# Batch 0 of a linear attention is loaded and attended by halves of its heads

## The chip, the cores and the metric

The kernel runs on one core of a Trainium2 chip. The metric is the device time of one execution in microseconds (us). Three runs of the kernel before took 282.03, 282.73 and 283.08 us; the median is 282.73.

A core has five engines, each with its own queue of instructions: PE (TensorE: matmuls, and transposes as matmuls with an identity), DVE (VectorE), ACT (ScalarE), POOL (GpSimd) and SP (SyncE, here only an issuer of transfers). 16 DMA engines move data between the chip's memory and the on-chip memory. PE writes to eight banks of accumulators (PSUM), from which DVE and ACT read.

## The reference

A linear attention with cosine weights, followed by a two-layer network with the gate h·cos(h):

```python
batch, n_heads, seq, head_dim = (8, 8, 576, 64)
theta = np.pi / 2.0 * pos / S
def phi(x, c, s):
    r = np.maximum(x, 0.0)
    return np.concatenate([r * c, r * s], axis=-1)
q_p, k_p = phi(q, cos_w, sin_w), phi(k, cos_w, sin_w)
kv = np.einsum('bhsf,bhsd->bhfd', k_p, v)
z = np.sum(k_p, axis=2)
num = np.einsum('bhsf,bhfd->bhsd', q_p, kv)
den = np.einsum('bhsf,bhf->bhs', q_p, z)[..., None] + 1e-06
x = (num / den)          # transposed to (4608, 512)
h = x @ w_in             # 512 x 2048
return (h * np.cos(h)) @ w_out   # 2048 x 512
```

All inputs and the output are float32; the kernel computes in float16 with float32 sums.

## The kernel before

**Tiles.** A batch has 576 tokens: four tiles of 128 (t = 0 to 3) and a fifth of 64, which is computed together with the fifth tile of the neighbouring batch. Batches 0 and 1 are attended at the start; the others are attended while the network works on the batch before them.

**Attention of one batch**, as helper functions put it. `load` brings one of q, k, v by two transfers on SP's queue (lines 339 and 342), for a slice of heads. `prep` makes one feature (g = 0 cosine, g = 1 sine) of one token tile, on ACT (line 364) or DVE (line 365). `q_pe` transposes the q features of a tile, one transpose a head (line 420), and copies the bank to `qT`. `cast_v` casts v to float16 beside a column of ones (lines 378, 379). `kv` sums k features times v over the five tiles, four heads in each of two banks (line 391), and copies the sums to `kvz` (lines 404, 406). `num` multiplies `qT` with `kvz` (line 450), copies the denominators to `den` (468, 470), and its `norm` takes a reciprocal and multiplies (474, 476). `x_pe` transposes the result (line 496) into `xT`, the input of the network.

**The network of batches 0 and 1.** `layer1` makes 16 groups of eight matmuls (line 542). Each group needs two of the four token tiles of `xT` (hf = 0: tiles 0 and 1; hf = 1: tiles 2 and 3) and one of four quarters of w_in. A sine on ACT (line 514) and a product on DVE (line 519) follow each group. Three banks are used in turn. `layer2_plain` (line 784) then multiplies with w_out, first the lower half of the rows for all four tiles, then the upper half. Later batches use a scheme with fewer matmuls (lines 685 and 849) and sums on DVE.

**Order.** Each step is recorded with an engine and the keys that it reads and writes. The table `KEYS` gives each step a place; the steps are issued in the order of that table, so each engine's order is fixed. A step that may go to two engines has its choice in the last digit.

**The front.** `first_attention` clears the fifth tiles, runs 14 filler matmuls (`warm`, line 917) while the loads run, loads q and k whole and v by halves of the heads, and attends the batch with 16 more filler matmuls between the transposes of q and `kv`, and 4, 3, 2, 0 after the tiles' sums. `weights` (on POOL) waits for k (`hold`, line 922), then issues w_in's quarters 0, 2 and 1, waits for quarter 0 (`hold2`, line 932), and issues one of w_out's lower quarters, w_in's quarter 3 and the other one of w_out. Batch 1's loads wait on SP for small casts on POOL (`hold_raw`, line 947), which wait for w_in's quarter 0 and for whoever still reads batch 0's raw tile. The upper half of w_out waits for batch 1's q (`part_of_w_out`, line 954).

Of the kernel before, what the change touches and what calls it, by code (L numbers as in the profile page):

```python
# [10 lines left out]
AF = mybir.ActivationFunctionType  # L11
ALU = mybir.AluOpType
# [181 lines left out]
def kernel(  # L194
# [9 lines left out]
    nc = tc.nc  # L204
    B, H, S, D = q.shape
    Dm, Dff = moe_w_in.shape
    P = 128
# [886 lines left out]
```

## Time and profile before

| | us |
|---|---|
| median of three runs | 282.73 |
| the profiled execution | 281.65 |
| its span, first to last instruction | 279.2 |
| PE busy | 269.7 |
| DVE busy | 250.3 |
| ACT busy | 218.6 |
| first matmul of layer 1, batch 0 | 21.69 |
| first matmul with w_out | 37.77 |

The profile is of one execution, with times from the start of its span. The slices of the span show the busy share of each engine in tenths. A line of the chain of waits has a start, a length and an engine with a line of the kernel. A line of the timeline has a start, a length, engine, line, operation, output<-input and a count; behind it, in brackets, the idle time before it and what ended that. The granted clock is the share of its full clock that PE was given.

### The profile page before, as it was taken

The numbers are of one execution on the slowest core, as the hardware profiler recorded it, in microseconds if no ns is written. First come the engines' busy times: TensorE is split into PE (matmuls) and PEld (weight loads), VectorE is DVE, ScalarE is ACT, GpSimd is POOL, SyncE is SP. The second block draws the span as 40 slices with busy tenths as digits, with TensorE's granted clock in tenths as the row PEclk, the third lists the DMA queues.
The fourth block names the chain that finished last, engine by engine and source line by source line (L and its number), as shares of the span: only waits on it lengthen the run. The fifth ranks groups of instructions, "written<-read, shape, count | busy, mean of one in ns | idle before, by whom it ended". The sixth has DMA issues, their size and how long they took to land.

```text
span 279.2 us, 6855 instructions
## 1 busy us (share of the span) xinstructions
PE 269.7 (97%) x2715; PEld 218.8 (78%) x2715; DVE 250.3 (90%) x449; ACT 218.6 (78%) x401; POOL 8.4 (3%) x21
## 2 busy tenths in 40 slices
PE   7789999999999999999999999999999999999994
PEld 2558767769856778789879887998788888888883
DVE  2678699999999999999999999999999999998872
ACT  2756698799999999999999999984684686777210
POOL 1340020000000000000000000000000000000000
PEclk9799999999999999999999999999999999999999
DMA  6999999979999999999799999747210400200324
GB/s 199 316 196 252 250 319 268 338 201 171 332 300 245 241 251 273 308 218 260 233 283 233 285 252 243 155 78 206 40 39 4 188 2 0 77 0 2 150 79 150
DMA packets 77599, 53.30 MB, mean 191 GB/s; under 512 B 46080, under 2 KB 75264, under 8 KB 77568
## 3 DMA queue, kind: packets, MB, share of 16 engines
q1 hardware_dynamic: 72608, 48.12, 65.3%
q0 software_dynamic: 4224, 4.19, 9.1%
q10 hardware_dynamic: 736, 0.57, 0.6%
q8 instruction: 21, 0.34, 0.5%
q14 instruction: 10, 0.08, 0.1%
HBM read 36.74 MB, written 9.44 MB: 165 GB/s over the span
## 4 chain that ended last, share of the span: by engine, by line
PE 91%; DMA 3%; ACT 2%; DVE 2%; issue 0%; SPq 0%; ACTq 0%
PE M L849 34%; PE M L685 16%; PE M L542 10%; PE M L582 9%; PE TR L685 6%; PE M L784 5%; PE ATT L450 3%; PE ATT L391 3%; DMA km<-in_k_dram 3%; PE TR L582 1%; PE M L420 1%; ACT KQ L364 1%; PE M L917 1%; PE M L496 1%; ACT V L378 1%; DVE gT L519 1%
## 5 line engine op out<-in xcount | busy, mean ns | idle before, releaser
L514 ACT ACTIVATE ch<-M 128x512 f32<-128x512 f32 x90 | 54.0, 604 | 14.0 <-PE M L685 6.8
L849 PEld LDWEIGHTS <-gT 128*128 128x128 f16 x560 | 54.1, 98 | 8.2
L519 DVE TENSOR_TENSOR gT<-M,ch 128x512 f16<-128x512 f32 x84 | 55.8, 683 | 4.4 <-ACT ch L514 4.1
L849 PE MATMUL M<-w_out_sb,gT 128*128 128x256 f16 x448 | 56.4, 272 | 0.0
L364 ACT ACTIVATE KQ<-km,CS 128x512 f16<-128x512 f32 x56 | 39.0, 734 | 0.5 <-DMA km<-in_k_dram 0.5
L364 ACT ACTIVATE KQ<-qm,CS 128x512 f16<-128x512 f32 x48 | 33.5, 728 | 4.9 <-DMA qm<-in_q_dram 4.9
L685 PEld LDWEIGHTS <-w_in_sb 128*128 128x128 f16 x320 | 31.0, 98 | 4.6 <-issue 0.2
L849 PE MATMUL M<-T,S 128*128 128x256 f16 x256 | 31.5, 272 | 0.0
L318 ACT ACTIVATE ost<-M 128x512 f32<-128x512 f32 x32 | 19.3, 602 | 15.0 <-PE M L849 9.5
L542 PE MATMUL M<-xT,w_in_sb 128*128 128x256 f16 x256 | 30.1, 273 | 0.6 <-DVE gT L519 0.5
L542 PEld LDWEIGHTS <-w_in_sb 128*128 128x128 f16 x256 | 24.6, 98 | 4.8 <-issue 1.2
L582 PE MATMUL M<-xT,w_in_sb 128*128 128x512 f16 x112 | 27.9, 379 | 0.0
L849 PEld LDWEIGHTS <-S 128*128 128x128 f16 x256 | 24.9, 98 | 3.3
L476 DVE TENSOR_TENSOR x<-ATT,rec 128x512 f16<-128x512 f32 x32 | 22.1, 691 | 2.5
L685 PEld LDWEIGHTS <-WS 128*128 128x128 f16 x216 | 20.6, 98 | 2.6
L582 PEld LDWEIGHTS <-w_in_sb 128*128 128x128 f16 x128 | 11.9, 98 | 9.2
L365 DVE TENSOR_SCALAR KQ<-qm,CS 128x512 f16<-128x512 f32 x32 | 14.2, 477 | 5.5 <-DMA qm<-in_q_dram 5.5
L450 PEld LDWEIGHTS <-qT 128*128 128x128 f16 x320 | 14.8, 98 | 3.5 <-issue 1.4
L323 DVE TENSOR_TENSOR S<-gT 128x2048 f16<-128x2048 f16 (+1 forms) x16 | 17.2, 1082 | 0.0
L323 DVE TENSOR_TENSOR gT<-Z,ch 128x1024 f16<-128x1024 f32 x13 | 15.8, 1217 | 0.3 <-ACT ch L707 0.2
L450 PE MATMUL ATT<-kvz,qT 128*128 128x65 f16 x288 | 15.3, 194 | 0.4 <-DVE kvz L406 0.4
L698 DVE TENSOR_TENSOR Z<-M,Z 128x512 f32<-128x512 f32 x22 | 14.9, 685 | 0.7 <-PE M L685 0.2
(138 smaller groups left out, 450.3 us busy)
## 6 DMA issues: line engine op xcount, KB each, us to landing
out_dram<-ost SPq DMA_DIRECT2D x33, 256.0 KB, 2.8
qm<-in_q_dram SPq DMA_DIRECT2D x8, 640.0 KB, 5.8
km<-in_k_dram SPq DMA_DIRECT2D x8, 640.0 KB, 5.8
qm<-in_q_dram SPq DMA_DIRECT2D x8, 512.0 KB, 5.7
km<-in_k_dram SPq DMA_DIRECT2D x8, 512.0 KB, 5.9
vm<-in_v_dram SPq DMA_DIRECT2D x6, 640.0 KB, 7.3
vm<-in_v_dram SPq DMA_DIRECT2D x6, 512.0 KB, 6.3
w_in_sb<-in_moe_w_in_dram POOLq DMA_DIRECT2D x4, 512.0 KB, 8.7
```

The costliest lines, as they stand in the source:

```text
L318: "ACT": lambda: nc.scalar.activation(out=out_, in_=in_, func=AF.Copy),
L323: return lambda: q.tensor_tensor(out=out_, in0=in0, in1=in1, op=op)
L364: fn = {"ACT": lambda: nc.scalar.activation(out=out_, in_=in_, func=AF.Relu, scale=sc), "DVE": lambda: nc.vector.tensor_scalar(out=out_, i ...
L450: nc.tensor.matmul(bank[hb][:, hh * D1:(hh + 1) * D1], lhsT=a[:, h, :], rhs=z[:, h, :], start=(i == 0), stop=(i == len(parts) - 1))
L476: nc.vector.tensor_tensor(out=split(x16[n][:, hs, :], k), in0=A[:, :, :, 0:D], in1=split(rec[n][:, hs], k).unsqueeze(3).broadcast_to((P, k ...
L514: act(0.5, due, lambda: nc.scalar.activation(out=ch[c], in_=bank, func=AF.Sin, bias=math.pi / 2.0, scale=1.0), [key], [("ch", c)])
L519: dve(0.61, due, lambda: nc.vector.tensor_tensor(out=dst, in0=a, in1=b, op=ALU.mult), [key, ("ch", c), *rd], dkeys)
L542: nc.tensor.matmul(M1[m][:, jj * 2 * P:(jj + 1) * 2 * P], lhsT=w_in_sb[:, cc, j * P:(j + 1) * P], rhs=X[:, cc, ts], start=(jj == 0 and cc ...
L582: nc.tensor.matmul(M, lhsT=w_in_sb[:, cc, j * P:(j + 1) * P], rhs=X[:, cc, :], start=(cc == 0), stop=(cc == NCT - 1))
L685: nc.tensor.matmul(bank[0][:, j * TH:(j + 1) * TH], lhsT=a(cc, j), rhs=b[:, cc, :], start=(first and j == 0 and cc == 0), stop=(last and j ...
L698: dve(0.61, due + 0.3, lambda: nc.vector.tensor_tensor(out=dst, in0=bank[0], in1=dst, op=ALU.add), [bank[1], key], [key])
L849: nc.tensor.matmul(bank[0][:, tt * MH:(tt + 1) * MH], lhsT=a[:, j, tt * P:(tt + 1) * P], rhs=b[:, j, :], start=(first and (apart or tt == ...
```

## The change

Batch 0's heads are treated in two halves (0 to 3, then 4 to 7). q, k and v are loaded by halves, all three of the first half ahead of the second: 12 transfers in place of 8. Features, transposes of q, copies, casts of v (two token tiles in one instruction now), sums, norms and transposes of x are done for each half; a tile's two halves of x go to two banks. POOL's hold of w_in reads the second half of q in place of k. The filler matmuls become 14 and 14, and 3, 2, 0, 0. The keys of `qT`, `x16` and `xT` get a half, so that a step waits only for the half that it reads. `layer1` could take a group in two parts, but `PARTS` is 0, so it does not. The three clears at the start share a key and so keep the order q, k, v. The table `KEYS` is new throughout. In it, w_in's quarters come in the order 0, 1, 3, then `hold2`, quarter 2 and both lower quarters of w_out, and only then the cast for which batch 1's k waits. The last of the 16 groups of layer 1 comes after w_out's first tile.

```diff
-    FILL = (4, 3, 2, 0)
+    FILL = (3, 2, 0, 0)
+    WARM0, PARTS = (14, 14), 0
...
+    def num_half(t, hb, bank, key, due):
+        n, hs = t, HALVES[hb]
+        full[key] = False
+        def mm():
+            for hh in range(HB):
+                h = hb * HB + hh
+                nc.tensor.matmul(bank[:, hh * D1:(hh + 1) * D1], lhsT=qT[t][:, h, :],
+                                 rhs=kvz[0][:, h, :], start=True, stop=True)
+        pe(HB, MMA, due, mm, [("qT", t, hb), ("kvz", 0, hb)], [key])
...
+        def norm():
+            nc.vector.reciprocal(out=rec[n][:, hs], in_=den[n][:, hs])
+            nc.vector.tensor_tensor(
+                out=x16[n][:, hs, :], in0=A[:, :, 0:D],
+                in1=rec[n][:, hs].unsqueeze(2).broadcast_to((P, HB, D)), op=ALU.mult)
+        dve(0.62, due, norm, [key, *dk], [("x16", n, hb)])
...
-                in_=raw[ORDER0[1]][0:1, 0, 0, 0:1].broadcast_to((1, 4)))
-        pl.add("POOL", 0.4, 0.5, 0, hold, hk(ORDER0[1]), [("w_in", g) for g in range(4)])
+                in_=raw[ORDER0[0]][0:1, HB, 0, 0:1].broadcast_to((1, 4)))
+        pl.add("POOL", 0.4, 0.5, 0, hold, hk(ORDER0[0], range(HB, H)), [("w_in", g) for g in range(4)])
...
-        warm(14, 6.5)
-        for nm in ORDER0:
-            load(0, nm, 0, HALVES if nm == ORDER0[2] else (slice(0, H),))
+        warm(WARM0[0], 0.2157 * WARM0[0] + 3.4)
+        for hs in HALVES:
+            for nm in ORDER0:
+                load(0, nm, 0, (hs,))
         weights()
+        for hb, hs in enumerate(HALVES):
+            for t in range(NT):
+                for g in range(2):
+                    prep(0, "q", t, g, "", t, hs)
+                q_pe(0, t, *BANKS[t], "ACT" if t % 2 else "DVE", t, hb)
+            if hb == 0:
+                warm(WARM0[1], 0.2157 * WARM0[1], rd=[("TR", 0)])
+            for t in range(NT + 1):
+                for g in range(2):
+                    prep(0, "k", t, g, "", 4, hs)
+            for t, nt in ((0, 2), (2, 2), (4, 1)):
+                cast_v(0, t, "", 5 + hb, hs, nt)
+        kv(0, 7, BANKS2)
+        pair = [((ATT[:, hb, :], ("ATT", hb)), BANKS2[hb]) for hb in range(2)]
         for t in range(NT):
...
+            for hb in range(2):
+                bank = pair[hb][t % 2]
+                num_half(t, hb, *bank, 8 + t)
+                fill = FILL[t] if hb else 0
+                if fill:
+                    warm(fill, 0.2157 * fill, M1[1], [bank[1]], [("M1", 1), ("fill", t)])
+                x_pe(0, t, t, *(BANKS[3], BANKS[2])[hb], "ACT", 8 + t,
+                     [("fill", t)] if fill else [], hb)
```

More of the change, by code (lines that the diff above doesn't have):

```diff
@@ L403, in kv @@
         if pair:
-            act(0.4, due, lambda: nc.scalar.activation(
-                out=Z[:, 0], in_=bank[0][:, 0:HB * D1], func=AF.Copy), keys[:1], zk[:1])
-            dve(0.4, due, lambda: nc.vector.tensor_copy(
-                out=Z[:, 1], in_=bank[1][:, 0:HB * D1]), keys[1:], zk[1:])
+            for hb in range(2):
+                copies(due, {"ACT": 0.34, "DVE": 0.36}, Z[:, hb], bank[hb][:, 0:HB * D1],
+                       keys[hb:hb + 1], zk[hb:hb + 1], 1)
         else:
@@ L411, in qdst, with q_pe @@
     def qdst(b, t):
-        return (qT[t], ("qT", t)) if t < NT else (qT4[b % 2], ("qT4", b % 2))
-    def q_pe(b, t, bank, key, eng, due):
+        dst, nm = (qT[t], ("qT", t)) if t < NT else (qT4[b % 2], ("qT4", b % 2))
+        return dst, [(*nm, hb) for hb in range(2)]
+    def q_pe(b, t, bank, key, eng, due, hb=None):
         dst, dkey = qdst(b, t)
         ps = bank.bitcast(F16).rearrange("p (h s) -> p h s", h=H)
+        hs = slice(0, H) if hb is None else HALVES[hb]
+        heads = range(H)[hs]
+        if hb is not None:
+            dkey = dkey[hb:hb + 1]
         def mm():
-            for h in range(H):
+            for h in heads:
                 nc.tensor.matmul(ps[:, h, :], lhsT=qp[:, t, h].rearrange("p g d -> p (g d)"),
@@ L422, in q_pe @@
         full[key] = False
-        pe(H, MMT, due, mm, [("qp", t, g, h) for g in range(2) for h in range(H)] + ["ID"], [key])
-        copies(due, {"ACT": 0.95, "DVE": 0.69}, dst, ps, [key], [dkey], 1 if eng == "ACT" else 2)
+        pe(len(heads), MMT, due, mm, [("qp", t, g, h) for g in range(2) for h in heads] + ["ID"],
+           [key])
+        copies(due, {"ACT": 0.95, "DVE": 0.69} if hb is None else {"ACT": 0.55, "DVE": 0.4},
+               dst[:, hs], ps[:, hs], [key], dkey, 1 if eng == "ACT" else 2)
     def q_dma(b, t, due):
@@ L440, in num @@
         parts = [(qdst(b, t)[0], kvz[b % 2])]
-        rd = [qdst(b, t)[1]] + [("kvz", b % 2, i) for i in range(2)]
+        rd = qdst(b, t)[1] + [("kvz", b % 2, i) for i in range(2)]
         if t == NT:
             parts.insert(0, (qT4[1 - b % 2], kvz[1 - b % 2]))
-            rd += [("qT4", 1 - b % 2)] + [("kvz", 1 - b % 2, i) for i in range(2)]
+            rd += qdst(1 - b, t)[1] + [("kvz", 1 - b % 2, i) for i in range(2)]
         def mm(hb):
@@ L479, in norm, with x_pe @@
                     op=ALU.mult)
-        dve(0.9 if pair is None else 1.02, due, norm, keys + [("den", n, h) for h in range(H)], [("x16", n)])
-        return n
+        dve(0.9 if pair is None else 1.02, due, norm, keys + [("den", n, h) for h in range(H)],
+            [("x16", n, hb) for hb in range(2)])
+        return n
+    def num_half(t, hb, bank, key, due):
[7 more added lines that the diff above has]
+        pe(HB, MMA, due, mm, [("qT", t, hb), ("kvz", 0, hb)], [key])
+        A = bank[:, 0:HB * D1].rearrange("p (h d) -> p h d", h=HB)
+        dk = [("den", n, h) for h in range(H)[hs]]
+        either(due, {"DVE": 0.09, "ACT": 0.07}, {
+            "ACT": lambda: nc.scalar.activation(out=den[n][:, hs], in_=A[:, :, D], func=AF.Copy,
+                                                bias=1e-6),
+            "DVE": lambda: nc.vector.tensor_scalar_add(out=den[n][:, hs], in0=A[:, :, D],
+                                                       scalar1=1e-6)}, [key], dk)
+        def norm():
[4 more added lines that the diff above has]
+        dve(0.62, due, norm, [key, *dk], [("x16", n, hb)])
     def xdst(b, t):
         if t < NT:
-            return xT[b % 2][:, :, t * P:(t + 1) * P], ("xT", b % 2, t)
+            return xT[b % 2][:, :, t * P:(t + 1) * P], [("xT", b % 2, t, hb) for hb in range(2)]
         i = b // 2
-        return xR[:, :, i * P:(i + 1) * P], ("xR", i)
-    def x_pe(b, t, n, bank, key, eng, due, after=()):
+        return xR[:, :, i * P:(i + 1) * P], [("xR", i)]
+    def x_pe(b, t, n, bank, key, eng, due, after=(), hb=None):
         dst, dkey = xdst(b, t)
@@ L492, in x_pe @@
         x2 = x16[n].rearrange("p h d -> p (h d)")
+        cs, xk = slice(0, NCT), [("x16", n, i) for i in range(2)]
+        if hb is not None:
+            cs = slice(hb * NCT // 2, (hb + 1) * NCT // 2)
+            dkey, xk = dkey[hb:hb + 1], xk[hb:hb + 1]
         def mm():
-            for c in range(NCT):
+            for c in range(NCT)[cs]:
                 nc.tensor.matmul(ps[:, c, :], lhsT=x2[:, c * P:(c + 1) * P], rhs=IDENT,
@@ L498, in x_pe @@
         full[key] = False
-        pe(NCT, MMT, due, mm, [("x16", n), "ID", *after], [key])
-        copies(due, {"ACT": 0.5, "DVE": 0.4}, dst, ps, [key], [dkey], 1 if eng == "ACT" else 2)
+        pe(len(range(NCT)[cs]), MMT, due, mm, [*xk, "ID", *after], [key])
+        copies(due, {"ACT": 0.5, "DVE": 0.4} if hb is None else {"ACT": 0.3, "DVE": 0.24},
+               dst[:, cs], ps[:, cs], [key], dkey, 1 if eng == "ACT" else 2)
     def x_dma(b, t, n, due):
@@ L505, in x_dma @@
             out=dst, in_=x16[n].rearrange("p h d -> p (h d)"), transpose=True),
-            [("x16", n)], [dkey], dma=(131.0, 140.0, 26))
+            [("x16", n, i) for i in range(2)], dkey, dma=(131.0, 140.0, 26))
     m1n, chn, m2n = [0], [0], [0]
@@ L547, in layer1 @@
                         full[("M1", m)] = True
-                        pe(2 * NCT, MMH, due, mm, xk[2 * hf:2 * hf + 2] + [("w_in", quarter)]
-                           + ([("a21", j0 // 2 - JH // 2)] if j0 >= JH else []),
-                           [("M1", m)])
+                        parts = [range(NCT)]
+                        if c == 0 and n <= PARTS:
+                            parts = [range(NCT // 2), range(NCT // 2, NCT)]
+                        for cs in parts:
+                            hb = range(2) if len(parts) == 1 else [cs[0] * 2 // NCT]
+                            pe(2 * len(cs), MMH, due, lambda mm=mm, cs=cs: mm(cs=cs),
+                               [("xT", c, t, i) for t in (2 * hf, 2 * hf + 1) for i in hb]
+                               + [("w_in", quarter)]
+                               + ([("a21", j0 // 2 - JH // 2)] if j0 >= JH else []),
+                               [("M1", m)])
                         gate(M1[m], ("M1", m), G[:, j0:j0 + 2, ts],
@@ L620, in tt @@
         def tt(n, a, b, op, rd, wr):
-            q = [("qT", n // 4)] if g >= OWN and n > 1 else []
+            q = [("qT", n // 4, hb) for hb in range(2)] if g >= OWN and n > 1 else []
             sums(due, CH2 * GW, ws[n], a, b, op, [("w_in", g // 2), ("w_in", 2 + g // 2)] + rd,
@@ L962, in first_attention @@
             dve(0.53, i - 9, lambda nm=nm: nc.vector.memset(raw[nm][:, :, NT, :], 0.0), [],
-                [((nm, h), 0) for h in range(H)])
-        warm(14, 6.5)
-        for nm in ORDER0:
-            load(0, nm, 0, HALVES if nm == ORDER0[2] else (slice(0, H),))
-        weights()
-        for t in range(NT):
-            prep(0, "q", t, 0, "DVE", t)
-            prep(0, "q", t, 1, "DVE" if t == 1 else "ACT", t)
-            q_pe(0, t, *BANKS[t], "ACT" if t % 2 else "DVE", t)
-        warm(16, 3.45, rd=[("TR", 0)])
@@ L973, in first_attention @@
-        for t in range(NT + 1):
-            prep(0, "k", t, 0, "DVE", 4)
-            prep(0, "k", t, 1, "DVE" if t == 2 else "ACT", 4)
-        for hb in range(2):
-            for t in range(NT + 1):
-                cast_v(0, t, "ACT" if t % 2 else "DVE", 5 + hb, HALVES[hb])
-        kv(0, 7, BANKS2)
-        for t in range(NT):
-            num(0, t, 8 + t, PAIRS0[t % 2])
-            if FILL[t]:
-                warm(FILL[t], 0.2157 * FILL[t], M1[1],
-                     [(("ATT", "M2")[t % 2], 1)], [("M1", 1), ("fill", t)])
-            x_pe(0, t, t, *BANKS[3 - t % 2], "ACT", 8 + t, [("fill", t)])
+                [((nm, h), 0) for h in range(H)] + ["zero"])
```

13 lines of the change are left out of this document (7 added, 6 removed), and 245 rows, old and new, of the table KEYS.

## The prediction

> **What bounds the kernel now.** First view: the profile's slices, then the busy times over chosen stretches.
>
> ```profile
> PE   7789999999999999999999999999999999999994
> DMA  6999999979999999999799999747210400200324
> ...
> 6.30:8.80 2.50, 0.05 (x2) 0.05 (x2) 0.80 (x2) 0.82 (x2) 0.00 (x0) 0.92 1.04 325
> 8.80:21.70 12.90, 11.88 (x138) 8.37 (x139) 9.58 (x27) 8.88 (x19) 5.73 (x12) 0.88 1.10 243
> 21.70:37.80 16.10, 15.45 (x145) 13.37 (x145) 12.34 (x25) 11.13 (x19) 1.28 (x3) 1.00 1.15 270
> 37.80:60.00 22.20, 22.20 (x243) 15.11 (x241) 21.08 (x50) 19.90 (x43) 0.42 (x1) 1.00 0.97 268
> 60.00:275.20 215.20, 215.09 (x2181) 180.20 (x2179) 204.62 (x346) 176.40 (x319) 0.00 (x0) 1.00 0.69 174
> ```
>
> Columns: stretch, length, then PE, PEld, DVE, ACT, POOL busy, granted clock, DMA share, GB/s. From 21.7 us on, PE idles 0.65 + 0.00 + 0.11 us. So the end is set by when batch 0's first layer starts; before that PE only does attention and filler matmuls. The DMA engines are full from 3 us to about 57 us all the same: data can become the limit as soon as PE comes sooner.
>
> Second view: the chain of waits in the front.
>
> ```profile
> 3.35 7.95 DMA km<-in_k_dram
> 11.38 1.62 ACT KQ L364 x3
> 15.27 0.92 ACT qT L318
> 16.27 1.38 PE M L391 x40
> 18.70 1.51 PE M L917 x7
> 21.69 1.03 PE M L542 x8
> ```
>
> All of q lands first (8.0, when DVE and ACT begin), all of k at 11.3, v last. kv starts at 16.27, layer 1 at 21.69. The engines idle until 8.0 and then have two tensors' features, copies and casts in front of kv.
>
> Third view: transfers, with median us from issue to landing, and the issues on POOL and SP in order of time.
>
> ```profile
> w_out_sb<-in_moe_w_out_dram POOLq DMA_DIRECT2D x1, 512.0 KB, 16.9
> ...
> 20.15 0.74 POOL L942 DMA_DIRECT2D w_out_sb<-in_moe_w_out_dram  x1
> ...
> 18.09 0.60 SPq L342 DMA_DIRECT2D km<-in_k_dram  x1
> 24.89 0.60 SPq L339 DMA_DIRECT2D qm<-in_q_dram  x1
> 32.37 1.37 SPq L339 DMA_DIRECT2D vm<-in_v_dram  x1
> ```
>
> The first-half w_out of 20.15 lands at 37.05; PE first uses it at 37.8. Batch 1's last q (13.4 to landing) is there at 38.3, its last v (9.1) at 41.5.
>
> **The change, part by part.**
>
> Loads. 8 issues become 12, q, k, v of heads 0 to 3 and then of 4 to 7; bytes and runs are the same. Issues take 0.63 to 0.89 us each on SP, so 12 take about 8.2 us from 0.73: the last leaves SP at about 9. A half tensor is 0.59 MB, 1.7 us at the 345 GB/s of these stretches; two issues are 1.3 us, so SP does not limit. Data flows from 2.95, and k (2.36 MB in order, so 9.8) landed at 11.3: 1.5 us behind its bytes. So the halves land at 6.2, 7.9, 9.6 and 11.3, 13.0, 14.5. The last v is no sooner than now; what is gained is that half the work is done by then. The memsets now go q, k, v, so the first gated q load leaves 0.5 us sooner; hidden behind nothing, worth under 0.5 us on the first half only.
>
> POOL. The hold of w_in waits for the fourth half (q's second, 11.3) in place of k (11.3): w_in starts as now. Order: w_in 0, 1, 3, the second hold, w_in 2, w_out 1, w_out 0, and only then the hold behind which batch 1's k waits (0.74 us each: k's issue moves from 18.1 to about 21). w_in 2 comes fourth and is wanted at 27; the fourth transfer landed at 28.0 with k beside it, and at 2.5 us a quarter it would land at 25 alone. Wait 0 to 1; I take 0, since k now starts after most of it.
>
> Vector and scalar work. Features go from 18 instructions to 36, qT copies from 4 to 8, v casts from 10 to 6, norms, den and x copies double. By rows: a DVE 128x512 feature is 478 ns, the 128x256 cast 279; on ACT 706 and 402. Two halves cost 0.08 to 0.1 us over a whole, about 2 us over both engines, nearly all while loads run. Without that cover it would be 1 us an engine.
>
> Path after the last landing at 14.5. ACT casts three of the five tiles: 0.40 + 0.70, two halves pitch to 15.5. kv of the second half, 20 matmuls, half of 1.38: 16.2. Two half qT copies stand ahead on ACT (0.6 each, 0.5 pitch): 16.5; kvz 0.39: 16.9. Two num halves 0.13 each and latency: 17.2. den 0.18: 17.45. Norms of 0.6 (reciprocal 0.2, product 0.42, pitch less): 18.1, 18.7, den 0.15, the third 19.45. Layer 1 stands on PE behind tile 2's transposes (0.15): 19.75. That is 1.9 sooner than 21.69. Bounds: 19.3 (nothing ahead of kvz) to 21.7 (below, clock). The last norm (two more, 20.65), its transposes and a copy behind a sine on ACT let the third group start at 22.1, now 24.2: 2.1 sooner.
>
> PE then. 13 groups of 0.87 and late q's transposes of 0.6 bring PE to w_out at 34.1. w_out 0 lands between 30 (six quarters at 2.56 us from 14.1, alone, plus latency) and 37.05 as now. As k shares only from about 22, I take 34.5: 0.4 wait. PE then leads by about 1.9.
>
> Second attention, where I give time back. Its data have the same bytes ahead of them in full engines, so q lands near 38.3 and v near 41.5, as now. Rows:
>
> ```profile
> 39.29 1.94 ACT L364 ACTIVATE KQ<-qm,CS 128x512 f16<-128x512 f32 x3
> 42.83 0.71 ACT L378 ACTIVATE V<-vm 128x256 f16<-128x256 f32 x2
> 42.20 1.29 DVE L379 CAST V<-vm 128x256 f16<-128x256 f32 x6
> ```
>
> The headroom is 1.0 us for q (38.3 to 39.3) and 0.7 to 1.3 for v. So ACT and DVE, busy 4.00 of 4.00 us from 40 to 44, can move ahead by 1.0, not 1.9; PE waits for them. Bounds: 1.9 kept, or data later by all of k's 3 us (below).
>
> Later the order table is rewritten. PE idles 0.11 us of 215, so a new order cannot win there; DVE is busy 95%, so it can lose. Bounds 0 and 1.0; I take 0.5.
>
> Sum: -1.0 + 0.5 = -0.5 us. The profiled execution took 281.65 (span 279.2, 2.45 around it), so 281.15; it lies 1.1 under the median 282.73, so the median goes to **282.2**.
>
> **A rule weighed.** Between 6.31 and 8.76 PE had nothing; the granted clock fell to half from 8.45 and came back at 11.86, while PE ran only transposes:
>
> ```profile
> 5.03:8.45 3.42, 1.28 (x6) 0.39 (x4) 0.45 (x2) 0.47 (x1) 0.00 (x0) 0.99 1.03 338
> 8.45:11.86 3.41, 3.10 (x30) 3.11 (x31) 2.31 (x6) 2.88 (x5) 0.21 (x2) 0.51 1.04 351
> 15.27:18.69 3.42, 2.40 (x59) 1.94 (x58) 1.88 (x7) 1.47 (x3) 0.68 (x3) 1.00 1.24 206
> ```
>
> A stretch with 1.28 us of PE work lost the clock, one with 2.40 kept it. The change puts about 1.6 us of scattered transposes and small matmuls into 11.9 to 15.3, in between. The Trainium skill, "TensorE: Matmul & The Clock Gate", Part 4 (PE-mode transpose), says that transposes don't count as PE work for this clock; by that, the stretch would hold well under 1 us and go cold, and the time would be the second rival's 282.8 in place of 282.2. The trace differs: 30 transposes at 0.51 stand before the return to 1.00.
>
> **Rivals.**
> - *All is kept.* Headroom of q and v is no limit because the transfers finish sooner, w_out being out of the way. For it: PE had work of other kinds at 38 to 52. Against: the same bytes. 282.73 - 1.9 = 280.8.
> - *The clock falls at 15.3.* At half clock kv's half takes 0.69 more and two nums 0.27: layer 1 at 20.7, with fillers up to 21.7. The lead at w_out shrinks from 1.9 to 0 to 0.9: from -0.4 to +0.5 after the later loss; 282.8. For: 1.6 lies nearer to 1.28 than to 2.40. Against: the gaps between matmuls are near 1 us, not 2.4.
> - *Slower: batch 1's loads come late.* One mechanism, on POOL and SP: k's issue waits 3 us behind three weight transfers, and the engines don't make it up. Then v lands at up to 44.6, the casts end 0.9 later, and kv's second half starts at 45.5, now 44.6; with the 7 us from there to layer 1 unchanged, that and the later loss make +1.4, more if k holds up features too: 284.4. It decides from v landing after 43.5 (no gain), and beyond 44.5 it is a loss one for one. For: SP's v issues of 2 to 2.6 us show full queues. Against: a full queue serves the same bytes in the same time.
> - *Nothing happens*, since the last v lands as now, would give 282.7; the work left after 14.5 speaks against it and it lies within the forecast's own range.
>
> **Numbers.** Forecast 282.2, 0.45 (own range 281.3 to 283.2); all kept 0.20; clock 0.11; late loads 0.24. Changes under 0.5% (1.4 us) can hardly be told from none here. Faster by more (under 281.3): most of all-kept and the forecast's edge, 0.23. Slower (over 284.1): most of late loads and the clock's edge, 0.23. The rest, 0.54. The range reaches from all-kept's 280.8 to 284.6.
>
> **What would show it.** Features from 6.2 to 6.4; the last v cast before 15.8; kv's second half near 15.6; layer 1 near 19.8; the clock 1.00 from 12 on; w_out waited for under 1 us; batch 1's last v at 41.5 and kv at 42 to 43; PE idle after 21 us grown from 0.76 to over 1.5. I am wrong if layer 1 starts after 21, if PE has no idle in 34 to 48, or if v lands after 43.5.

## The result and the profile after

The changed kernel took 283.38 us (median of 20 runs, 282.37 to 285.72) beside 282.18 for the kernel before (20 runs): ratio 1.0047, 95% interval 1.0029 to 1.0066, so some 1.3 us slower. Its profiled execution took 282.76 (span 281.0), that of before 281.65 (span 279.2). Executions that take over 1.5% more than the fastest of the same kernel are left out, which are three of the twelve of e7 below, its profiled one among them.

The slices and the same stretches of the changed kernel (columns as in the prediction):

```profile
PE   8769999999999999999999989999999999999993
...
6.30:8.80 2.50, 2.50 (x25) 1.68 (x24) 0.03 (x2) 1.18 (x4) 0.00 (x0) 1.00 0.96 320
8.80:21.70 12.90, 8.54 (x119) 5.84 (x117) 11.66 (x46) 9.91 (x26) 5.61 (x12) 1.00 1.05 239
21.70:37.80 16.10, 15.51 (x137) 12.57 (x135) 12.44 (x22) 11.63 (x21) 0.31 (x3) 1.00 1.15 265
37.80:60.00 22.20, 21.96 (x242) 15.31 (x241) 20.61 (x52) 19.56 (x37) 1.74 (x3) 1.00 0.99 274
60.00:277.00 217.00, 215.47 (x2182) 180.23 (x2180) 206.08 (x348) 176.45 (x318) 0.00 (x0) 1.00 0.69 173
```

The front now holds 8.54 us of PE work where it held 11.88, and DVE is busy 11.66 of 12.90. But behind 60 us PE stands idle 1.53 us, where it stood idle 0.11; the one 8 late in PE's slices is the slice from 161.6 to 168.6 us. The waits of PE from 20 us on, in the changed kernel (in total, times, longest):

```profile
PE ATT L460 <- DMA qT<-KQ: 0.8, 1, 0.8
PE M L536 <- ACT xT L322: 0.6, 2, 0.3
PE M L832 <- DMA w_out_sb<-in_moe_w_out_dram: 0.4, 1, 0.4
PE M L733 <- ACT M L322: 0.3, 1, 0.3
PE ATT L460 <- ACT kvz L322: 0.2, 1, 0.2
```

The longest is late in the run, for a transposed q of batch 6. To place the time I took, for each two successive matmuls, the distance of their starts less the usual distance for that shape; what is left is PE's idle time. One profiled execution of each kernel, in us:

| | before | changed | changed front, old order |
|---|---|---|---|
| first matmul of layer 1 | 21.68 | 21.26 | 22.02 |
| idle from there to 38 | 1.20 | 1.26 | 1.70 |
| idle 38 to 60 | 0.10 | 0.79 | 0.09 |
| idle 60 to 135 | 0.24 | 0.55 | 0.44 |
| idle 135 to 165 | 0.59 | 1.36 | 0.59 |
| idle after 165 | 0.08 | 0.35 | 0.09 |
| PE's work | 251.10 | 250.88 | 250.89 |
| from PE's end to the span's end | 4.21 | 4.55 | 3.99 |

(The third column is the first experiment below.) In the changed kernel the front gained 0.42 us in place of 1.9; the rest lost 2.1 us of idle time and 0.3 at the end.

Why the front gained so little, in the timeline of the changed kernel (start, length, engine, line; in brackets idle time and what ended it):

```profile
8.78 0.62 DVE L369 TENSOR_SCALAR KQ<-km,CS 128x256 f16<-128x256 f32 x2 [2.48 <-DMA km<-in_k_dram]
...
16.02 0.42 DVE L383 CAST V<-vm 128x512 f16<-128x512 f32 x1
...
16.49 0.98 PE L395 MATMUL M<-V,KQ 128*128 128x65 f16 x20 [0.55 <-DVE V L383]
...
18.33 0.29 PE L501 MATMUL ATT<-kvz,qT 128*128 128x65 f16 x4 [0.56 <-DVE x L514]
...
21.26 1.03 PE L583 MATMUL M<-xT,w_in_sb 128*128 128x256 f16 x8
```

The first half of k landed at 8.7 us, forecast 7.9; DVE then worked without a gap until 17.5, at 0.27 us between half features, and came to its last v cast at 16.02 (forecast: before 15.8). The first numerator of the second half was ready with `kvz` at 17.90, but started at 18.33: it writes one bank of the tile ATT while DVE still reads the other one (`norm2` of the first half).

Of issues, on POOL and SP:

```profile
20.07 1.50 POOL L990 DMA_DIRECT2D w_out_sb<-in_moe_w_out_dram  x2
...
21.74 0.60 SPq L346 DMA_DIRECT2D km<-in_k_dram  x1
34.20 1.48 SPq L343 DMA_DIRECT2D vm<-in_v_dram  x1
```

Batch 1's k is issued 3.6 us later than before, its last v 1.8, yet `kv` of batch 1 starts at 43.26, before at 43.84.

### The profile page after: what moved, and what is told of

Read it like the earlier page. It is cut to its first block, busy times and chain, and to the rows that moved or that the text cites. A ratio compares the mean times of both kernels' runs of the same rounds, so it can differ in the third digit from the quotient of the medians.

```text
span 281.0 us, 6889 instructions
## 1 busy us (share of the span) xinstructions
PE 269.0 (96%) x2709; PEld 217.5 (77%) x2709; DVE 253.6 (90%) x474; ACT 221.4 (79%) x406; POOL 8.6 (3%) x21
## 4 chain that ended last, share of the span: by engine, by line
PE 52%; ACT 4%; DMA 2%; DVE 2%; issue 1%; ACTq 0%
PE M L897 26%; PE M L733 13%; PE TR L733 5%; PE M L630 3%; DMA qT<-KQ 2%; PE ATT L460 1%; PE ATT L395 1%; ACT KQ L368 1%; PE TR L630 1%; ACT ch L555 1%; ACT ost L322 1%; DVE gT L560 1%; ACT V L382 0%; DVE gT L327 0%; DVE S L327 0%
## 5 line engine op out<-in xcount | busy, mean ns | idle before, releaser
L555 ACT ACTIVATE ch<-M 128x512 f32<-128x512 f32 x90 | 52.9, 601 | 12.5 <-PE M L583 5.8
L368 ACT ACTIVATE KQ<-qm,CS 128x512 f16<-128x512 f32 (+1 forms) x55 | 36.8, 702 | 2.2 <-DMA qm<-in_q_dram 2.2
L368 ACT ACTIVATE KQ<-km,CS 128x512 f16<-128x512 f32 (+1 forms) x54 | 36.1, 705 | 1.7 <-DMA km<-in_k_dram 1.7
L322 ACT ACTIVATE ost<-M 128x512 f32<-128x512 f32 x30 | 18.1, 604 | 15.0 <-PE M L897 9.3
L486 DVE TENSOR_TENSOR x<-ATT,rec 128x512 f16<-128x512 f32 x30 | 20.8, 692 | 2.1
L369 DVE TENSOR_SCALAR KQ<-km,CS 128x512 f16<-128x512 f32 (+1 forms) x36 | 14.0, 424 | 2.5 <-DMA km<-in_k_dram 2.5
L369 DVE TENSOR_SCALAR KQ<-qm,CS 128x512 f16<-128x512 f32 (+1 forms) x33 | 13.7, 447 | 2.7 <-DMA qm<-in_q_dram 2.7
L755 ACT ACTIVATE ch<-Z 128x1024 f32<-128x1024 f32 x14 | 14.9, 1065 | 1.5 <-DVE Z L746 1.5
L327 DVE TENSOR_TENSOR gT<-Z,ch 128x1024 f16<-128x1024 f32 x13 | 15.8, 1219 | 0.1
L460 PEld LDWEIGHTS <-qT 128*128 128x128 f16 x288 | 13.3, 98 | 3.3 <-DMA qT<-KQ 1.1
```

The costliest lines, as they stand in the source:

```text
L322: "ACT": lambda: nc.scalar.activation(out=out_, in_=in_, func=AF.Copy),
L327: return lambda: q.tensor_tensor(out=out_, in0=in0, in1=in1, op=op)
L368: fn = {"ACT": lambda: nc.scalar.activation(out=out_, in_=in_, func=AF.Relu, scale=sc), "DVE": lambda: nc.vector.tensor_scalar(out=out_, i ...
L369: "DVE": lambda: nc.vector.tensor_scalar(out=out_, in0=in_, scalar1=0.0, scalar2=sc, op0=ALU.max, op1=ALU.mult)}
L460: nc.tensor.matmul(bank[hb][:, hh * D1:(hh + 1) * D1], lhsT=a[:, h, :], rhs=z[:, h, :], start=(i == 0), stop=(i == len(parts) - 1))
L486: nc.vector.tensor_tensor(out=split(x16[n][:, hs, :], k), in0=A[:, :, :, 0:D], in1=split(rec[n][:, hs], k).unsqueeze(3).broadcast_to((P, k ...
```

## The experiments

"Early" times and orders are places in the table `KEYS`, in us of its own plan. All kernels were timed beside the kernel before, and a ratio is to that. "Layer 1" is the start of its first matmul, and the last three columns are of one profiled execution each. Idle matmuls are fillers whose results nobody reads; those of e5 and later are described with e5.

| kernel | median (runs) | ratio, 95% interval | layer 1 | idle behind it | of it 135 to 165 |
|---|---|---|---|---|---|
| e1 new front, old order | 281.45 (12) | 0.9966 [0.9946, 0.9987] | 22.02 | 2.9 | 0.59 |
| e2 old front, new order | 285.42 (6) | 1.0119 [1.0080, 1.0158] | 22.31 | 6.5 | 3.29 |
| e3 changed, `norm2` later | 283.50 (10) | 1.0042 [1.0018, 1.0066] | 21.30 | 5.7 | 2.40 |
| e4 changed, two issue queues | 284.33 (10) | 1.0067 [1.0038, 1.0096] | 23.29 | 5.3 | 2.91 |
| e5 e1, idle matmuls, `norm2` later | 282.10 (12) | 0.9989 [0.9964, 1.0013] | 22.01 | 3.9 | 0.60 |
| e6 e5, two features on ACT | 283.44 (12) | 1.0038 [1.0006, 1.0070] | 21.74 | 4.4 | 0.68 |
| e7 changed, old order from 140 on | 284.19 (9) | 1.0059 [1.0035, 1.0083] | - | - | - |
| e8 changed, old order up to 60 | 285.97 (6) | 1.0116 [1.0073, 1.0159] | 21.20 | 8.7 | 3.72 |
| e9 changed, three steps back | 283.52 (12) | 1.0065 [1.0037, 1.0093] | 20.49 | 4.7 | 1.51 |
| e10 e1, idle matmuls | 283.10 (12) | 1.0039 [1.0007, 1.0071] | 20.69 | 5.6 | 0.60 |
| e11 e10, w_in's last quarter sooner | 280.69 (12) | 0.9958 [0.9933, 0.9984] | 21.20 | 4.0 | 0.66 |
| e12 e10, hold reads v | 281.02 (12) | 0.9968 [0.9945, 0.9991] | 21.29 | 3.8 | 0.58 |
| e13 e11 and e12 | 280.55 (6) | 0.9920 [0.9890, 0.9951] | 21.16 | 3.0 | 0.79 |
| e14 before, w_in's last quarter sooner | 282.05 (12) | 0.9965 [0.9940, 0.9990] | 22.11 | 2.8 | 0.58 |
| e15 e11 without idle matmuls | 281.41 (12) | 0.9963 [0.9937, 0.9990] | 20.89 | 2.9 | 0.60 |
| e16 e14, more idle matmuls | 282.02 (12) | 0.9998 [0.9972, 1.0024] | 21.03 | 3.4 | 1.04 |
| e17 e13 again | 281.03 (12) | 0.9959 [0.9934, 0.9983] | 21.69 | 2.8 | 0.58 |
| e18 changed order, front of e13 | 284.77 (6) | 1.0100 [1.0065, 1.0135] | 21.63 | 5.6 | 3.17 |

**Front or order?** The table gives all places anew, so the first two runs cross them: the steps of the first attention from one kernel, the places of everything behind it, and of the weights on POOL (six places that the cuts below leave out), from the other.

```diff
-KEYS = after[:129] + after[129:]
+KEYS = after[:129] + [k + 0.57 us for k in before[90:]]
```

> The changed front, with everything after batch 0's attention and the transfers of weights in the order of the kernel before. Theory A: the loss lies in the rewritten order of the rest, so PE's idle time after the first layer-1 matmul falls from 4.3 us back to about 2.3 us, the front's gain of 0.4 us stays, and the time is 0.2 to 0.5 us below the kernel before (ratio 0.998 to 0.999). Rival B: the halved front itself disturbs what follows (its data, its phase against the transfers), whatever the order: idle time stays near 4 us and the ratio near 1.005.

```diff
-KEYS = before[:90] + before[90:]
+KEYS = before[:90] + [k - 0.57 us for k in after[129:]]
```

> The reverse: the front of the kernel before, unsplit, with the weights' order and all that follows in the order of the changed kernel. Theory A: slower than the kernel before by 1.3 to 2.0 us (ratio 1.005 to 1.007), PE idle 4 us after layer 1 starts, with a wait for a transposed q of batch 6 near 161 us. Rival B: same as the kernel before, ratio 1.000.

e1 is faster than both kernels, e2 slower than both: the split front with the old order gains 1.0 us, and the new order costs 1.9 us behind the new front (283.38 against 281.45; 2.3 by the two ratios) and 3.4 behind the old one, more than the 1.3 to 2.0 expected. The loss is the rewritten order's, not the split's. The gain of e1 is seen in its runs and not in its profile: the two profiled executions took 281.68 and 281.65 us, and layer 1 starts at 22.02 there, before at 21.68. Which wait it saves stays open.

Where in the order? Three runs tried to divide it, by half tables and by three steps.

```diff
-KEYS = after
+KEYS = after below 140 us, before + 0.57 us from 140 us on
```

> The changed kernel, with the order of before (shifted by 0.57 us) for all steps that are planned from 140 us on; everything earlier as changed. It splits the 1.9 us that the rewritten order costs. If PE's extra idle time in the profile is the cost, the stretch from 135 us on holds 0.8 of it (1.37 against 0.59 us between 135 and 165): the time falls from 283.38 to about 282.6 (ratio about 1.002). If the loss is all in the second attention and the stretch around 100 us, it stays at 283.3; if all is behind 140 us, 281.5.

```diff
-KEYS = after
+KEYS = before + 0.57 us where that is below 60 us, after otherwise
```

> The other half of the split: the split front, the order of before for all steps that it plans before 60 us (the weights' loads, the second attention) and the changed order behind it. The idle time of the changed kernel between 44 and 50 us (0.80 against 0.10 us) should go: about 282.7 (ratio 1.002). If the second attention's order costs nothing in the end because the later stages wait anyway, 283.3; if it is the whole loss, 281.5.

```diff
-prep q2 g0 153.22, prep q2 g1 153.84, q_dma t2 154.66
+prep q2 g1 149.30, prep q2 g0 150.30, q_dma t2 151.45
```

> The changed kernel with three steps of batch 6 moved back to about where the order of before had them: the two features of q's third block on ACT, planned 153.22 and 153.84, go to 149.30 and 150.30 (behind one sine of layer 1, ahead of the next), and the transposing DMA that they feed from 154.66 to 151.45. In the changed kernel's profile this transpose and the next run together for 4.11 us and PE waits 0.81 us for them (0.97 of idle time at 161.83). Theory K (the rewritten order costs what its own stalls of PE show): that idle time goes, and the time falls by 0.5 to 1.0 us, to 282.4 to 282.9. Rival L (the stall only passes on, PE is late elsewhere since ACT's sines come later by two features of 0.8 us): PE's idle time between 145 and 165 us stays at 1.3 us or more, and the time stays within 0.3 us of 283.4 or rises.

Neither half gives a price. e7 (1.0059) is not told from the changed kernel (1.0047), though it has the order of before from 140 us on, and e8 is slower than the changed kernel (1.0116); none of the outcomes expected came (281.5 to 283.3). Why a mixture gains nothing stays open. What the profiles do show is a wait that comes with the new order. In the changed kernel, e2, e3, e4, e8 and e18, which all have it in that place, PE waits 0.8 to 2.3 us for a transposed q at 162 to 167 us; in the profile of before and the eleven with the unmixed old order (e1, e5, e6 and e10 to e17) there is one such wait, of 0.4 us. The changed kernel, then e8:

```profile
162.80 0.43 PE L460 MATMUL ATT<-kvz,qT 128*128 128x65 f16 x8 [0.81 <-DMA qT<-KQ]
```

```profile
165.51 0.62 PE L440 MATMUL ATT<-kvz,qT 128*128 128x65 f16 x8 [2.30 <-DMA qT<-KQ]
```

e9 took away this wait of the changed kernel, its longest (0.97 us of idle time at 161.8 became 0.17 at 164.5), and the time stayed (1.0065 against 1.0047): rival L. In its timeline PE now waits two us after the features that were moved forward, on DVE's features of the same tile:

```profile
153.71 1.03 PE L877 MATMUL M<-w_out_sb,gT 128*128 128x256 f16 x8 [0.33 <-DVE KQ L349]
```

So this one wait is not the price of that order; what can be shown is the stretch. In the table's last column the new order has 1.4 to 3.3 us of idle time from 135 to 165 us (changed kernel 1.36), behind five different fronts (the changed one, the old one, and those of e3, e4 and e18), and the unmixed old order 0.6 to 1.0. The closest test is e18, beside e17, with all of the front's mends:

```diff
-KEYS = after[:129] + [k + 0.57 us for k in before[90:]]
+KEYS = after[:129] + after[129:]
```

> The changed kernel with its own rewritten order behind the front, and the same three edits in the front as the best kernel has (idle matmuls, the hold on the first half of v, w_in's last issue ahead of the hold for w_out). If the rewritten order is what loses, it stays 1.5 to 3 us above the best kernel: 282.0 to 283.5, with PE's idle time at 44 to 50, 103 and 161 us as in the changed kernel. If its loss was the late weights or the clock, 280.3 to 281.2.

The longest waits of PE in e18:

```profile
PE M L877 <- ACT ost L302: 1.3, 1, 1.3
PE ATT L440 <- DMA qT<-KQ: 1.0, 1, 1.0
```

Layer 1 starts at 21.63 in e18 and 21.69 in e17, PE's work is 250.88 in both, and the spans differ by 3.4 us: 2.8 of idle time and 0.6 at the end. With the front equal, the order, the weights' places with it, costs this: 3.7 us by the medians, more than the 283.5 at most that was expected. The two waits are for a copy on ACT and for a transposing transfer, not for a load. Why the new order makes them is not shown.

**The front's own stalls.** Two edits of the changed kernel: the wait for the neighbouring bank, and the late landing (are SP's 12 issues the limit?).

```diff
-den2 h0 15.79, norm2 h0 16.01
+den2 h0 16.42, norm2 h0 16.45
```

> The changed kernel, with the denominators and norm of tile 2's first half issued after the matmuls of tile 0's second half, so that these do not wait for DVE to have read the neighbouring bank; each engine's own order is unchanged. Theory C: that wait (0.56 us of idle PE at 17.8) is 0.4 us on the path: the matmuls start at 18.0 in place of 18.3, layer 1 at 20.9 in place of 21.26, the time is 0.1 to 0.4 us below the changed kernel (ratio to the kernel before 1.003 to 1.004). Rival: DVE is the limit anyway, layer 1 stays at 21.2 to 21.3.

```diff
             def go4(h=h, four=four):
-                nc.sync.dma_start(out=blocks(m, 1 - n)[:, h, 0:NT, :], in_=four)
+                q4.dma_start(out=blocks(m, 1 - n)[:, h, 0:NT, :], in_=four)
+            q4 = nc.scalar if b == 0 and (nm, h.start) in (("k", 0), ("v", 0)) else nc.sync
```

> The changed kernel, with two of the twelve loads (four-token parts of the first half of k and v) issued on ACT's queue before its table is loaded, so that all the others leave SP up to 1.3 us sooner. Theory D: the transfers run dry at 4 to 6 us (250 GB/s where the kernel before had 347) because twelve issues of 0.66 us feed them too slowly; then that stretch comes back to 320 to 350 GB/s, the first half of k lands near 8.1 in place of 8.7, the last v near 14.5 in place of 15.0, and layer 1 starts 0.5 us sooner, at 20.7 (time 0.3 to 0.5 below the changed kernel). Rival: half-sized transfers are slower in themselves, or fewer engines serve them: landings and layer 1 unchanged within 0.2 us.

In e3 the numerator follows `kvz` at once (17.46 us), so the wait was for the reader of the other bank; but the clock fell, layer 1 came at 21.30, and the time (1.0042) is not told from the changed kernel's. From 16 to 19 us:

```profile
16.00:19.00 3.00, 2.96 (x35) 2.11 (x33) 1.32 (x6) 0.96 (x4) 1.29 (x5) 0.50 1.24 204
```

In e4 the first half of k was there no sooner (its features start at 9.49), from 4 to 8 us the transfers ran at 277 GB/s against 284 in the changed kernel and 345 before. One profile each, this speaks against SP's issue as the limit. The same 12 loads let the features of k start at 8.78, 8.36 and 7.79 us in the changed kernel, e1 and e3; what sets that stays open.

The clock had fallen in three of these four profiles with the split front (e1, e3, e4). So idle matmuls of 128x512 go into PE's gaps:

```diff
+        for n in (3, 3, 5):
+            warm(n, 0.2157 * n, M2[1], (), [("M2", 1)])
         kv(0, 7, BANKS2)
```

> The split front with the order of before behind it (281.45 us, 0.9966 of before), and two edits in the front: den2 and norm2 of the first half go behind the numerators of the second half (the 0.38 us wait of a numerator for a reader of the neighbouring bank), and three groups of idle matmuls of 128x512 (3, 3 and 5 of them) are put into PE's gaps between 10.6 and 16 us, in the bank that kv's second half takes later. Theory F (what is left of the front's loss is the clock, which fell to 0.50 at 16 to 20 us in the profile of that kernel, and the bank wait): the clock stays at 1.00 from 12 to 20 us, layer 1's first matmul comes at about 20.6 us instead of 22.02, the second attention gives part of it back, and the time is 280.6 to 281.1. Rival G (the second attention's loads and features set the pace after layer 1 has begun): layer 1 starts as early, PE's idle time between 22 and 50 us grows by as much, and the time stays within 0.2 of 281.45. Rival H (the idle matmuls stand in front of late features' consumers): kv's second half starts later than 16.5 us and the time is above 281.7.

> The split front with the order of before behind it, and the idle matmuls in PE's gaps, without the move of den2 and norm2 (which in the profile of the kernel that had both put norm2 0.8 us ahead of norm0 of the second half on DVE, so that layer 1 started at 22.01 in spite of a clock of 1.00). Expected: clock 1.00 from 8 to 22 us, layer 1 at 21.2 us. Theory M (behind the front the loads set the pace: DMA is at a share of 1.1 to 1.25 from 16 to 36 us, and w_in's last quarter, issued behind a hold, came 1.0 and 1.7 us late for PE in the two kernels with idle matmuls): PE waits 0.8 to 1.8 us for w_in at 32 to 36 us, and the time stays at 281.4 to 282.1. Rival F (the front's gain reaches the end): that wait is under 0.3 us and the time is 280.6 to 281.0.

They do keep the clock: in the eight kernels that have them, 77 of 84 runs have a mean clock of 0.996 or more, 2 of 12 in e1. Alone they do not help: e5 is not told from before, e10 is slower than e1 (1.0039 against 0.9966). In e5 the moved `norm2` now ran ahead of `norm0` of the second half, and layer 1 stayed at 22.0. In e10 layer 1 started at 20.69, and PE met the next load. Its timeline:

```profile
31.54 1.03 PE L563 MATMUL M<-xT,w_in_sb 128*128 128x256 f16 x8 [0.54 <-DVE gT L540]
35.09 2.14 PE L563 MATMUL M<-xT,w_in_sb 128*128 128x256 f16 x18 [2.51 <-DMA w_in_sb<-in_moe_w_in_dram]
```

That is theory M: behind the front, w_in's last quarter, issued at 20.25 behind a hold and one w_out load, lands at 35.1; the wait is longer than the 0.8 to 1.8 expected, and so is the time. The idle matmuls have a part in it. In all eight kernels with them the hold for w_out was released 6.7 to 8.2 us after w_in's first issue, in the others 5.6 to 6.2; in e11 and e15 below, which differ in them alone, it took from 12.38 to 19.10 and from 12.14 to 18.08 (one profile each). Why is not shown.

In e6, moving features to ACT brought layer 1 forward by 0.27 us, between the two theories, and the time rose by 1.3, which neither had: 0.7 is this wait, which grew from 1.0 to 1.7; the rest is open:

```diff
-prep k0 g1 h0 7.51 DVE, prep k1 g1 h0 8.85 DVE
+prep k0 g1 h0 7.65 ACT, prep k1 g1 h0 7.66 ACT
```

> The kernel with the idle matmuls, and two of the nine half features of the first half of k that DVE computed move to ACT, which stood idle from 9.28 to 10.33 us there (0.43 us each on ACT, 0.27 each between starts on DVE). Theory I (DVE sets the pace of the split front, busy without a gap from 8.78 to 17.5 us): the last v cast, kv's second half and layer 1's first matmul come 0.4 to 0.6 us sooner than in the kernel without this move, and the time falls by 0.1 to 0.5 us. Rival J (the landing of the last v, 14.2 and 15.0 us, sets it): they come within 0.2 us of where they were, and the time is the same within 0.2 us.

**The weights.** Two edits of e10, then both.

```diff
-w_in 3 18.49
+w_in 3 13.80
```

> The kernel with the idle matmuls only, and w_in's last quarter issued third-from-first, ahead of the hold for w_out, instead of behind it and one w_out load (about 14.5 us instead of 19.8). Theory M: PE's wait for w_in at 32 to 36 us goes; the bytes are the same, so w_out and batch 1's k come later by up to 0.5 MB at about 205 GB/s (2.5 us), and PE waits there instead; the time lies within 0.4 us of the kernel with the idle matmuls only, or up to 1 us above it. Rival (it was the order of the weights alone): no new wait, time lower by the wait that went, 0.5 to 1.5 us.

```diff
-                in_=raw[ORDER0[0]][0:1, HB, 0, 0:1].broadcast_to((1, 4)))
-        pl.add("POOL", 0.4, 0.5, 0, hold, hk(ORDER0[0], range(HB, H)), [("w_in", g) for g in range(4)])
+                in_=raw[ORDER0[2]][0:1, 0, 0, 0:1].broadcast_to((1, 4)))
+        pl.add("POOL", 0.4, 0.5, 0, hold, hk(ORDER0[2], range(HB)), [("w_in", g) for g in range(4)])
```

> The kernel with the idle matmuls only, and the hold that starts the weights reads the first half of v (landed at 9.3 and 10.15 us in the changed kernel) instead of the second half of q (11.0 and 11.9). The DMA engines, at a share of 0.4 to 0.6 from 13 to 15 us with 50 to 130 GB/s, fill that gap. Theory M: the weights and batch 1 come about 1.5 us sooner, PE's wait for w_in at 32 to 36 us falls by as much, while q1, k1 and v1 land up to 0.7 us later and layer 1 starts by as much later; time 280.5 to 281.5, 0.3 to 1.0 below the kernel with the idle matmuls only. Rival (the second halves' loads lose more to the weights than the stream gains): layer 1 later than 22.5 and the time above 282.

> Both edits of the weights together on the split front with idle matmuls and the order of before behind it: the hold reads the first half of v, and w_in's last quarter is issued ahead of the hold for w_out. If the weights' stream is what the front's gain runs into, and both edits only move the same stream, PE's wait for w_in is zero in both and the second edit adds little: 280.3 to 281.0, no more than 0.4 below the better of the two alone (280.69). If the gap of the DMA engines at 13 to 15 us is worth its length, 279.5 to 280.2.

> The best kernel so far once more (split front, idle matmuls, both edits of the weights, the order of before behind it), beside the control on the same chip: 280.3 to 280.9, ratio 0.990 to 0.995.

e11 takes the wait for w_in away, and nothing took its place but 0.5 us of short waits at 38 to 50:

```profile
30.80 0.71 PE L563 MATMUL M<-xT,w_in_sb 128*128 128x256 f16 x5
32.05 5.18 PE L563 MATMUL M<-xT,w_in_sb 128*128 128x256 f16 x46 [0.54 <-DVE gT L540]
```

That is 2.4 us below e10 on the same chip: of theory M, the late quarter holds, the new wait at w_out that it also expected does not. e12 halves the wait (1.2 us left). Both together have a median of 280.85 over 18 runs and were faster than before in each of two comparisons, but the second time (0.9959) above the 0.990 to 0.995 expected; they are not told from e11 (0.9958).

How much of this is the split's? Controls: the early quarter on the kernel before, e11 without idle matmuls, and the first control with more idle matmuls at the start.

```diff
-w_in 3 17.92
+w_in 3 12.60
```

> Control: the kernel before, with only w_in's last quarter issued ahead of the hold for w_out (planned 12.60 instead of 17.92). In its profile PE waits nowhere for w_in (the 0.5 at 32 us is for a product of DVE). If the early w_in is worth something only behind a sooner front, it is the same as before (ratio 0.999 to 1.001) or slower, since w_out and batch 1 come later; then the split front is what gains in the kernel at 280.69. If the early w_in is a gain of its own, it is faster by 0.5 us or more, and the split front is worth nothing.

> The kernel at 280.69 us without the three groups of idle matmuls. If the clock of the front matters behind the mended weights, the clock falls to 0.50 for about 3.4 us somewhere between 13 and 22 us in the profile, layer 1 starts 0.3 to 1.0 us later than 21.2, and the time is 281.0 to 281.5. If the front's chain of features and casts hides a slower PE, the same time within 0.3 us.

```diff
-        warm(14, 6.5)
+        warm(24, 6.5)
```

> Second control: the kernel before with w_in's last quarter issued early (282.05, ratio 0.9965) and 24 instead of 14 idle matmuls at the start, so that PE stays busy from 6.30 to about 8.5 us, where it stood idle and the clock fell for 3.4 us. If a clock of 1.00 in the front is worth something without the split, the 30 transposes at half clock take about 1 us less, layer 1 starts 0.3 to 0.8 us sooner (22.11 in the profile of the first control) and the time falls to 281.2 to 281.7; then less than 1 us of the 2.0 us of the best kernel (280.55) is left for the split. If k and v land too late for it to matter, 281.8 to 282.2, and the split keeps 1.5 us.

On the kernel before, the early quarter alone gains 0.35%, though PE waits nowhere for w_in in the profile of before; why is open. So a part of what the best kernels gain over before is not the split's. With the idle matmuls of e16 the clock stays at 1.00, layer 1 starts 1.1 us sooner (21.03 against 22.11), and nothing arrives at the end (0.9998; 1.2 us of waits for transposed q come later). On the same chips the split front with its mends is 0.45% below e14 and 0.39% below e16, some 1.2 us; the intervals overlap, and the controls keep the old hold. Among runs with a mean clock of 0.996 or more, e17 (12 runs) has a median of 281.03 and e16 (10) of 281.77, 0.7 us apart. That agrees in size with the 1.0 us of e1, and does not prove it. e15 is not told from e1 (0.9963 and 0.9966), so without idle matmuls no gain of the early w_in behind the split front is seen; the fall of the clock and the later layer 1 that were expected of it did not come in its profile (1.00, 20.89).

## Why the prediction was wrong

Forecast 282.2 from 282.73, a gain of 0.2% (half a us); measured, a loss of 0.47%.

- **The step that failed: "Later the order table is rewritten", bounds 0 and 1.0, taken 0.5.** e1 against the changed kernel gives 1.9 to 2.3 us, e2 3.4 by its ratio, e18 against e17 3.7. The sign and its reason (PE idle 0.11 of 215 us, so nothing to win) were right; the upper bound of 1.0 came from no row, and no row of the trace of before could show it, since the stalls are those of an order that had not run. Which steps of the new order cost it stays open.
- **The net of front and second attention, -1.0: right in size, by luck.** e1 is that part by itself: 0.9966, that is 1.0 us (0.4 to 1.5). The 2.3 us of the order, by the ratios, are what is between that and the measured 1.3. But neither of the two terms that gave -1.0 came as forecast, and the profile of e1 does not show where its gain lies.
- **The two terms.** Layer 1 at 19.75 was too early (its steps as written, 19.45 and 0.15, make 19.60): it came at 21.26, beyond the 21 that was named as a sign of being wrong. An estimate of the 1.5 us, from the rows above: some 0.85 is k's landing (284 GB/s, not the 345 that I carried over from the larger loads), up to 0.4 DVE's 0.27 us for a half feature in place of 0.22 to 0.24, and 0.38 the neighbouring bank. Other profiles with this front and no idle matmuls have it at 20.49 to 23.29. And the giving back by batch 1's q and v did not show: `kv` of batch 1 came 0.58 us sooner, so that the lead at layer 1 was kept to there. What a sooner front meets first is w_in's last quarter, which I had covered only as "0 to 1; I take 0" for quarter 2; for the last quarter of the old order, behind a layer 1 at 20.69 (e10), it was 2.5 us.
- **w_out, 0.4 us of wait:** 0.4 measured, by luck: PE was ready at 35.9 and w_out there at 36.3, forecast 34.1 and 34.5. (The lead behind it is 37.8 - 34.5 less one group of 0.87, that is 2.4 and not 1.9; the sum, which took 1.0, does not use it.)
- **The clock rival (0.11, 282.8):** in the changed kernel's profile the clock stayed at 1.00; in those of e1, e3 and e4, with the same front, it fell to 0.50 for some 3.4 us between 15 and 22 us. Over the 139 runs of the kernel before that stood beside the experiments, the median is 281.7 where the mean clock was 0.996 or more (41 runs), 282.4 at 0.990 to 0.996 (82), and 283.5 below (16). The profile of before, at 0.992, has one fall. So a fall goes with some 0.7 us, and before has it too in most of its runs, so it tells little between the two. e1 gains 0.8 to 1.0 us in the first two classes (2 and 10 runs), the changed kernel loses 1.2 to 1.4 in both.
- **The rule of the Trainium skill** ("TensorE: Matmul & The Clock Gate", Part 4) that transposes don't count as PE work: by it the stretch of scattered transposes would go cold. In the changed kernel it did not, and the traces do not bear the rule out. Below are stretches of 3.41 us, in whole steps from where the clock changes in each profile: e1, the changed kernel (whose clock changes at the end, at 278.68), then e4. PE's busy time stands behind the comma, the clock in the third column from the end.

```profile
12.93:16.34 3.41, 1.90 (x30) 1.42 (x29) 3.26 (x14) 3.41 (x9) 2.27 (x3) 1.00 0.75 154
16.34:19.76 3.42, 3.10 (x36) 2.34 (x37) 2.35 (x11) 2.29 (x8) 1.16 (x4) 0.50 1.24 206
```

```profile
12.44:15.86 3.42, 2.28 (x47) 1.89 (x44) 3.27 (x15) 3.42 (x10) 2.48 (x3) 1.00 0.69 149
15.86:19.27 3.41, 2.25 (x41) 1.65 (x39) 2.60 (x12) 2.35 (x8) 0.43 (x3) 1.00 1.24 205
```

```profile
12.22:15.64 3.42, 2.08 (x40) 1.60 (x40) 3.27 (x14) 3.11 (x9) 2.91 (x4) 1.00 0.63 175
15.64:19.05 3.41, 1.89 (x37) 1.60 (x38) 3.13 (x13) 2.65 (x7) 0.18 (x2) 1.00 1.14 186
19.05:22.46 3.41, 3.37 (x22) 1.81 (x23) 1.38 (x7) 1.41 (x6) 2.87 (x8) 0.50 1.24 208
```

The clock fell behind 1.90 and 1.89 us of PE work and stayed behind 2.28 and 2.08. Transposes are 1.68 of the changed kernel's 2.28 and 0.78 of e4's 1.89: without them the stretch that kept the clock has less work (0.60) than the one that lost it (1.11). The amount is not all either: in e4 a stretch of 1.73 us, nearly all idle matmuls (8.81 to 12.22), kept it. My estimate of 1.6 us for the change was too low.

- **Batch 1's loads late (0.24, 284.4):** the place was wrong. The issues moved as forecast (k from 18.1 to 21.7), and v was there in time: its casts run from 41.4 to 43.4, before from 41.1 to 43.5. The time came out on this rival's side by another way.

## What to carry to other kernels

When a change comes with a new order of everything behind it, price the two apart by crossing them before believing either: here a front worth 1.0 us lay under an order that cost 2. A stage that starts sooner is worth only what the next load in line allows, so look up when that load is issued and lands (w_in's last quarter) before adding the gain up. Half of an order need not bring half of its gain: of two mixtures of a good order with a bad one, neither was faster than the bad one and one was slower.

## What the runs showed of the hardware

The 12 loads of half size let their first reader of k start anywhere from 7.65 (e12) to 9.49 us (e4), and moved 256 (e11) to 313 GB/s (e17) from 4 to 8 us, where 8 larger loads moved 345 (before) to 366 (e16). A matmul into one bank of a two-bank tile waited 0.4 us for a DVE read of the other bank; whether the chip or the program's semaphores hold it there was not tried. The fall of the clock comes and goes from run to run of one program and lasts 3.41 us in the profiles; runs of the kernel before with a mean clock of 0.990 to 0.996 are 0.7 us longer than those above. With 11 idle matmuls in the front, the hold that waits for w_in's first quarter was released 6.7 us after that quarter's issue (e11), without them 5.9 (e15), one profile each.
